# A gated mix of attention and state-space convolution: the written order of all steps replaced by another order

## The chip, the cores and the metric

The kernel runs on one core of a Trainium2 chip. The metric is device time in microseconds (us). The engines are TensorE (PE; its weight loads are shown as PEld), VectorE (DVE), ScalarE (ACT), GpSimd (POOL) and SyncE (SP), whose queue issues all transfers here.

## The reference, cut to what matters

x is 2048 tokens of 512 values. `a` is an attention of 32 heads of 16 dims over four segments of 512 tokens, with a memory carried from segment to segment; `b` is a long convolution of x with a kernel that is computed from state-space parameters; a sigmoid gate for each token mixes them.

```
for s in range(4):                      # segments of 512 tokens
    p = softmax(qs @ ks.T * scale + mask);  a_dot = p @ vs
    a_mem = (phi(qs) @ M) / (phi(qs) @ z + 1e-6)
    o = g * a_mem + (1 - g) * a_dot
    M, z = M + phi(ks).T @ vs, z + sum(phi(ks))
a = concat(o) @ wo
K[d, l] = real(sum_n C[d,n] * exp(dt*A[d,n]*l) * dt*B[d,n])
b = irfft(rfft(x) * rfft(K)) + x * Dskip       # causal, padded to 2L
gate = sigmoid((x * gate_w).sum(-1))
return gate * a + (1 - gate) * b
```

## The kernel before

The kernel first builds a list of 1746 steps (`build_graph`, L525). Each step has a name (its tag), the engine that does it, the tiles that it reads and writes, and a function that emits its instructions. A step is one transfer, one ACT or DVE instruction, or a group of matmuls. Then `replay` (L235) walks through a text, `ORDER` (L368), that was written out beforehand. Each word of it is a step's number; a letter `a` or `v` says that an evacuation, which could be done by ACT or by DVE, is done by ACT or by DVE; the numbers after slashes are the slots of the tiles that this step takes first. `emit` (L264) gives each engine its steps in the order of the text and puts semaphore waits where a step needs another engine's result or a slot that another step must leave. Every engine works through its own list strictly in order, SP's queue of transfers too.

The work is in these parts, which the order interleaves:

* Start. Loads (`ld_*`), transposes of x (`xT0`, L709; later segments by a transposing transfer at L712), preparation of the state-space parameters (`ssm_prep`, L733), which begins with the exponential of `log_dt` on ACT (L750), and twenty powers of a complex vector by repeated squaring (`pow*`, `pwc*`, L784; squares on ACT at L794, sums and products on DVE at L795 and L796).
* Attention, for each segment s and each group hg of 8 heads: projections (`pk`, `pq`, L978), values (`tok`, L917), state of the memory (`st`, `sm`, L936), scores in five pieces (`sc`, L1007) whose exponentials run on ACT over four PSUM banks at once (L1068, 128 x 2048), masks on DVE (`mk`, L1080), products with the values (`pv`, 17 columns each, L1018), normalising (`nrm`, L1036), the memory's part (`mem`) and a transposed sum (`oT`, L1101).
* Tables of the convolution's kernel, for each quarter c of the channels (`tables`, L1137). Two tables F and G are built by complex products on DVE (`tab`, L1165, L1168, L1172) after copies of the first entries (`tabc`). Then the lag products (`lag0` to `lag3`, L1206) multiply them: eight steps for each quarter, each of 32 products of 20 columns with 32 weight loads of 32 columns, followed by two evacuations and four transfers into a table KT. F and G have one slot each (L628, L629), so the tables of the next quarter begin when the lag products of the last have read theirs.
* First level of x's transform (`xl1`, L844), evacuated mostly by ACT, and written to a scratch tensor in memory.
* Convolution in 32 units (`conv`, L1220): a load of constants (`CD`, c_DN in the profile, four slots), second level of x (`X`, loaded as `Zx`, with two swapping transfers), the kernel's transform from KT (`K`, five products of 512 columns), their product on DVE (`Y`, L1281), the inverse (`V`) and a transfer into V2.
* Finals, for 16 blocks of tokens (`finals`, L1297): `fin`, `fir`, `fih`, `fis` on PE, spilled parts (`spl`), and the outputs (`out`).

Evacuations are at L226 (ACT), L227 (DVE), L229 and L230 (with a scale). All matmuls but the transposes share line L686, and all transfers but the transposing ones share L222.

The two lines that make a lag step, and the two that give F and G their single slot:

```
FP = mkpool("F", 10240, 1)
GP = mkpool("G", 16384, 1)
...
i = mm(e, ap(P, sl * NF, n=NF, p0=32 * dq, np_=32), ap(G, (1 - cc) * GPL + (dl // 2) * 2 * NG + dl % 2, [[2, NG]]),
       ap(F, cc * FPL + (dl // 2) * 2 * NF + dl % 2, [[2, NF]]), cc == 0, cc == 1, tile_position=(0, 32 * dq))
```

Of the kernel before, what the change touches and what calls it, by code (L numbers as in the profile page):

```python
# [368 lines left out]
9/0 0/0 205/0 10/1 14/2 23/4/0 15/0 29/0 24v 38/0 54/0 39/1 31/2 30/3 21/0 37/4 12/3 13/4 55/0 33/5 34 35 57/5 36 32/6  # L369
44/7 17/0 40/8 41 377/0 42 45/9 20/0 56v/0 58a 43 11/5 48/0 27/1/1 46/10 47 1/0 49/11 53/0 61/1 50/12 200/6/0/0 62v/0  # L370
59/0 60 378/2 16/0 51/13 28v 52 25/7/2 201a 214/3/0/0 73/2 67/3 63 71/1 72 202 189/0 86v/1 83/2 85/4 22/0 18/0 196/0
197/0 26a 84 87 98v/2 203/1/0 97/5 3/0 95/3 250/4/1/1 253/0/1 74a/3 251a 215 204v 96 107/0 75 254a 240/0/0 99 110v/4
173/6 379 65/1 176/2 109/7 108 174/3 255/1/1/1 241 66 242 111 175/0 1247/1 178/0 77/0 121/2 78/4 119/1 7/0 120
293/2/2/2 179/3 76 193/0 995v/0 177 190 5/0 181/0 64 994v 219/0/1 220 191 88 996v 133/1 256 221 208/0 131/1 132 100
997v 1000/0 999 258 257 122a/5 998v/0 228/0/2 209a 229 210/0 79 206/1 1002 381/0 1003/1 143/2 192/0 198/0 1004 230
211a 144/5 216 145 112 1009/1 1008 158v/6 123 207a 159 1001 223/0/3 252 588/0 134a/7 135 1005 89/1 212/3 213v 294a 295
155/2 1011 1010 90/6 156/0 1226/0 224 225 146a/8 1250/0/0 1251a 799/0 199/0 800/1 157 222/2 1237/3/1 226 227 167a/9
1238a 231 2/0 266/0/1 267 268 801 1012/0 147 1013 1006/1 124 217 232/0 168 160 1020 91 1007 136 1015/0 1248/1 1249a
1014 1252 1021/1 337/0/2 338a 233 236/0/3 148 237 238 334/3/0/0 335a 1016 589/1 169 234/0 1234/0/0 590 1017 1022
1232/2 1018/0 235/1 1233a 1023 262/0/2 1235a 263 1236 264 239 243 101/1 244 1239/3 1240a 1229/2/0 1227/0 271/0/3 272  # L380
1024/1 245/1 1230a 1241 1019 273 1228a 1231 1025 1258/3/1 296/2/0 1026 297a 283/0/0 1259a 284 285 1033/0 1244/0/0
1245a 246 1032 1029 4/0 1034 265/2 1030/1 1035 1260/3 269 270 1261a 103/7 1031 380 279/0/2 280 281 1242/0 1243a
218/3/0 259 260/0 298/3/0/0 299 102 113/2 247 307/0/1 115/2 1036/0 1027/1 114 1262 1028 308 1037 278/0 282 286 287
1268/0 300 309 1246 248/1 249a/0 288/2 125/1 320/0/2 321 274 275/3 1038/1/0 1039 1040 126/1 127 322 137/2 1041 289
1043/3 194 290/1 276 1044 180 1045 1042a 1046 1047a 1263/0/1 1264a 1056v/0 1052v/0 1060 80v/0 339/1/1/1 1055v 138/5
340 1054v 301 1061/1 303/0/0 304 305 394/3/1 383/0/1/1 384a 341 1253/1/0 1254a 395a 324/0/3 342 1062 1053v 325 326 139
1058/0 81 1057 1066 336 302/0 343 400/1/0/0 401 1067/1 306/3 310 1059 311 277 1068 391 116a/2 344 1063 1070/0 346/0/0
1255/2 1073/1 1256a 1257 1069 1072 128v/3 347 348 1074 443/0/1 402 1050/0 1265/2 291/1 1266a 312/0/1 1064/1 292a 149/1
117 1071 444v 1079/0 1078 313 314 1267 349/2 386/0/0 1065 1080 1076/1 150/0 92a/4 490/1/2/2 182 315 316/4 93 387a 1049
1082/0 129 350/0/0 351 491a 398/0 352 82 1081 68a/5 1075 317 319/1 323 1083 152v/1 399a 1289/1 104a/6 355/0/1 356 357  # L390
1090 327 353 105 354 328 396/0 363/0/2 318/0 397a 385 140a/7 329/5 1091/0 330 364 365 358 1077 331 392/3 393a 1284/0/0
94 1286/1 1084 1092 1285a 106 1087 1094/1 367/0/0 368 359/0 1287a 369 1093 493/3/2 492 141 130 494a 1276/0/1 1277a
1085/0 405/0/3 1288 406 407 1095 151 440/1/0/0 441a 1088/1 1086 1297/3/0 1298a 362/0 360 1089 409/0/1 164v/9 410 161/3
118 411 448/1/1/1 366 370 371 372/1 195 1101/3/1 1102 449 373 1051 1103 1104 422/0/2 153 142 390/0 423 442 1105a 445/0
69 374/1 70 1295/3 1096/0 451 1097 450 1098 165 154 424 1296a 1099 361 1299 162/3 1274/1 1100a 1275a 403 426/0/0 427
1114v/0 428 166 163 375/2 1279/3/0 376a 1119/0 1280a 6/0 1281/0 1278 1111v/0 1282a 1118 261 408/1 1112v 412 414/0/3
447/1 1120 602/0 415 416 446 382/1 1113v 1271/2/1 1125/1 1110v 1124 404/3/1 609/0 1116/0 388/1 452 1115 1126 413 417
1117 170v/8 1121 1272a 464/0/1 1122/1 1131/0 171 172 1130 1127 1132 465 418/2 610a 421/2 425 429 1123 430 1128/0 1283
466 419 453 1129 1108 420/1 1269/0 1270a 1273 1292/3/0 1293a 1290/1 1291a 459/0/3 1136 460 431/3 541/0/0 461 542a
1137/1 986/0 1294 1134/0 1300/3/1 1301a 432 1307/1/0 1138 455/0/2 456 457 1133 1302/0 433 1303a 472/0/0 1304 473  # L400
1140/1 1139 1135 1141 1143/0 1308a 183/2 474 538/3/1/1 539a 498/0/0/0 1149/1 184/0 1148 1142 458/1 1150 499 500 462
1146/1 463 1144 1305/2 1306a 1145 1152/0 476/0/2 477 467 478 1151 332/3 333a 1147 1153 1309 468/4 607/2 608a 651/0/0/0
652a 520/0/3 345 469 521 522 471/3 1332/0 597/2/1 598a 475 479 480 1310/0 546/0/1/1 524/0/1 525 1048 547 548 470/0 501
1154/2/0 389 1311/1 549 1155 526 1156 1157 1158a 1106 484/0/5/0 507/0/0 508 481/1 1159/2 540 497/1 482 485 1160 483
495/0 496 486 1161 1162 487 509 1163a 1167 1172v/0 1170v/0 1176 1177/1 1165 434/0/0/1 435 1178 1166 436 1168a 1182
503/0/2 504 1171a 488/3 505 437 1312/2/0 1169v 1183/0 1313a 1173 591 1184 545/0 1174/1 1188 489a/0 1164 605/0 1339/1
506/1 606a 1175 1189/0 512/0/2 513 803 1179 1318/2 532/1/2/0 533 514 502/0 550 510 511 1185 1186/1 534 1187 599/1
562/0/0 563 592 1190 515 551 535 519/0 1368/2 523 1195/1 1194 543/0 516/3 564 603/2 604a 1321/3/1 1322a 1196 1191
570/0/2 571 572 517 438/2 1197 527 528 594/3/2/2 595a 1180/0 1198/1 1181 553/0/3 439a 554 555 1199 704/3/2 705a 1192/0
1314/2 1107 529/4 1315a 1316 1207/1 1193 557/0/1 558 559 1319/3 530 596 1109 1320a 531/0 611/2/0/0 1206 612 518 556/0  # L410
574/0/3 575 576 1208 560 1201/0 561 565 569/1 701/3/1/1 1200 566/1 1209 567 1202 616/0/1 573 1354/1 702a 577 578 568/1
1203 1210/1 1204/0 1211 1205 536/3 617 537a 653 1324 814/0/1 815a 620/0/0 816/3 654/0/0 621 655a 613 625/0/2 626
1212/0/0 1213 579/5 580 581 618 1214 1215 1216a 1325/2 1217/2 988/0 817v 1218 622 637/0/3 638 1219 1220 1221v 1326/1/2
1327v 1328/0 619/3 593/0 1329v 454 601/1 1223 659/2/1/1 660 661 627 623 633/0/1 634 818/1 819v 1426/0 752/0/1 753a 624
628 666/0/0 820/2 1447/1 703 629/0 635 630 667 749/1/2/2 750a 632/0 552 631/0 821v 670/0/2 671 544 582/1/2/1 614 639
583 584 585 636 640 641 662 642/4 615/1/0 658/0 731/0/1 656/0 732 657 672 643 668 1331 663 1330 644 1225 1222 1224
1448/2/0 664 1449v 709/3/0/0 687/0/3 695/0/3/0 710 711 1347/2 1433/2 586/2 696 697 1323 669/3 587v 698 688 751 706/0
707 1450/0 1317 1440/3 673 674 813 757/2/1/1 758 760 683/0/0 759 1441/0/1 684 802 1427/1/2 1428a 685 1442v 1451/2/0
1452a 708/0 1496/1 675/0/2 805/1/0/0 676 1434/0/3 1453/0 1435a 600 806a 1429/1 1443/2 1430/2/1 712 713/4 761 1454/0
1431a 1444/0/2 1445a 689 677 682/1 1350/5/1 1351a 1432 733 678 804/1 1348/2 1349a 686 1361/2 762 763 764/0/2 1446 690  # L420
1436/3 691 679/1 680 692/5 681/1 693 694 1353 1497/0/0 765 645/1/0/1 646 1498a 647 648 768/0/0 769 1335/1/0 1336v
808/0/0 809v 1437/2/3 1362/3/0 1438a 1333/1 1334a 1352 773/0/3 766 774 1363v 1461/3 1355/0/1 1356v 1475/2 649/2 650v/0
1455/1/2 987/1 767/3 1340/0 1456a 770 775 1337 1357/0 1338 1369/1 714/0/2 1358v 1499/0 715 1476/2/1 1477a 1457/1
1364/1 1365a 771 716 699/0 700a 1478/2 772 1390/2 776 1397/0 777/2 778 735/0/0 779/0 1439 1500/2/0 1501v 736 1462/1/3
1463v 1370/0/2 1371a 1479/3/1 1480v 1464/3 780/2 723/0/3 1458/1/2 1459v 1341/0/2 1342v 724 717/3 1343/1 1344a 781/0/2
1482/1 756/1 1483/0/0 725 730/1 734 1359 1468/2 737 738 782 1484v 754/1 1502 1367 1481 739 740/4 741 718/0/1 719 742/1
# [1003 lines left out]
```

## Time and profile before

| what | value |
|---|---|
| median of 3 runs | 317.85 us (317.22 to 318.82) |
| the profiled execution | 314.99 us, of it span 312.8 us |
| granted TensorE clock, mean | 0.947 |
| PE busy | 259.1 us, 4033 matmuls |
| DVE busy | 264.6 us, 641 instructions |
| ACT busy | 262.3 us, 313 instructions |
| matmuls of 20 columns (lag) | 1024, busy 10.2 us together |
| matmuls of 17 columns (pv) | 1280, busy 42.7 us together |
| exponential L1068, 128 x 2048 | 80, mean 1894 ns |

The span runs from the first to the last instruction; the rest of the execution's time lies around it. The page gives busy times of each engine, forty slices with the busy share of each in tenths, and a chain of waits, followed back from the last instruction, in which "issue" is time for which no semaphore accounts. A number in square brackets in the timeline is the idle time of the engine ahead of an instruction, with what ended it.

### The profile page before, as it was taken

The page shows a single profiled execution, that of the slowest core. Times are in us where ns is not written, and L with a number is a line of the kernel's source. Part 1 is how long each engine was busy: PE and PEld are TensorE (multiplying, and loading weights), DVE is VectorE, ACT ScalarE, POOL GpSimd, SP SyncE. Part 2 cuts the span into 40 slices and gives each one's busy share as a digit, 9 for nine tenths or more (in the row PEclk, how much of TensorE's full clock was granted, in tenths as well). Part 3 has the DMA queues.
Part 4 walks back from the last instruction along what each step waited for, and adds up shares of the span by engine and source line. Part 5 has one row for each costly group of instructions (what it writes and reads, how often), then busy time and mean ns, then how long its engine had stood idle before and what let it go on. Part 6 is the DMA issues. An engine that isn't in the chain of part 4 may idle for free.

```text
span 312.8 us, 9547 instructions
## 1 busy us (share of the span) xinstructions
PE 259.1 (83%) x4033; PEld 152.0 (49%) x4078; DVE 264.6 (85%) x641; ACT 262.3 (84%) x313; POOL 3.4 (1%) x9
## 2 busy tenths in 40 slices
PE   1595886658887687979796999999999999999993
PEld 0352443545445553556354655455544455546551
DVE  0799999959999899989996998997988898774473
ACT  2799999959999999899987899997899899986121
POOL 2000000000001000000000000000000000000000
PEclk9997899959999987999978899999999999999998
DMA  5956613400512331413030434675666767352133
GB/s 144 233 172 150 116 53 111 137 4 1 160 22 58 96 103 48 139 25 118 16 94 4 137 107 120 206 207 173 181 204 190 208 182 218 101 154 78 39 129 140
DMA packets 45002, 37.37 MB, mean 119 GB/s; under 512 B 21408, under 2 KB 40864, under 8 KB 44960
## 3 DMA queue, kind: packets, MB, share of 16 engines
q1 hardware_dynamic: 44960, 36.77, 40.7%
q8 instruction: 32, 0.52, 0.7%
q14 instruction: 10, 0.08, 0.1%
HBM read 18.54 MB, written 6.29 MB: 79 GB/s over the span
## 4 chain that ended last, share of the span: by engine, by line
PE 42%; ACT 25%; DVE 19%; DMA 6%; issue 5%; SPq 1%; ACTq 0%; DVEq 0%
PE psum L686 42%; ACT sb L1068 14%; ACT sb L226 7%; DVE sb L1165 5%; DVE sb L1168 4%; DVE sb L1172 4%; ACT sb L794 2%; DMA sb<-c_DN 2%; DMA sb<-sb 1%; DMA sb<-in_B_log_dt_dram 1%; DVE sb L227 1%; DMA scr_Z<-sb 1%; SPq L222 1%; ACT sb L802 1%; DVE sb L1043 1%
## 5 line engine op out<-in xcount | busy, mean ns | idle before, releaser
L686 PE MATMUL psum<-sb 128*128 128x17 bf16 (+11 forms) x3945 | 251.6, 230 | 39.9 <-ACT sb L1068 17.9
L686 PEld LDWEIGHTS psum<-sb 128*128 128x128 bf16 (+3 forms) x3990 | 144.8, 97 | 144.8 <-issue 33.5
L1068 ACT ACTIVATE sb<-psum 128x2048 bf16<-128x2048 f32 x80 | 151.5, 1894 | 7.1 <-PE psum L686 6.3
L226 ACT ACTIVATE sb<-psum 128x512 bf16<-128x512 f32 (+2 forms) x149 | 84.4, 613 | 17.1 <-PE psum L686 15.4
L227 DVE CAST sb<-psum 128x512 bf16<-128x512 f32 (+1 forms) x53 | 35.7, 683 | 11.2 <-PE psum L686 9.5
L1165 DVE TENSOR_TENSOR sb<-sb 128x512 bf16<-128x512 bf16 (+3 forms) x52 | 33.8, 660 | 0.0
L1168 DVE TENSOR_TENSOR sb<-sb 128x512 bf16<-128x512 bf16 (+3 forms) x52 | 33.6, 657 | 0.0
L1172 DVE TENSOR_TENSOR sb<-sb 128x512 bf16<-128x512 bf16 (+3 forms) x52 | 33.5, 659 | 0.0
L1080 DVE TENSOR_TENSOR sb<-sb 128x1024 bf16<-128x1024 bf16 (+1 forms) x40 | 22.3, 575 | 2.8 <-ACT sb L1068 2.8
L1281 DVE TENSOR_TENSOR sb<-sb 128x1024 bf16<-128x1024 bf16 x32 | 21.6, 684 | 0.7 <-issue 0.3
L229 ACT ACTIVATE sb<-psum,sb 128x512 f32<-128x512 f32 (+1 forms) x9 | 5.8, 686 | 9.6 <-PE psum L686 9.6
L1043 DVE TENSOR_TENSOR sb<-psum,sb 128x256 bf16<-128x256 f32 x32 | 13.3, 418 | 0.3
L794 ACT ACTIVATE sb<-sb 128x512 f32<-128x512 f32 x18 | 11.5, 647 | 0.0
L1040 DVE RECIPROCAL sb<-psum 128x16 f32<-128x16 f32 x32 | 8.0, 252 | 3.0 <-PE psum L686 2.8
L227 DVE COPY sb<-sb 128x256 bf16<-128x256 bf16 x18 | 4.9, 287 | 5.6 <-PE psum L686 5.6
L948 ACT ACTIVATE sb<-psum 128x512 bf16<-128x512 bf16 x12 | 7.4, 616 | 2.4 <-PE psum L945 2.4
L230 DVE TENSOR_SCALAR sb<-psum,sb 128x512 bf16<-128x512 f32 (+1 forms) x7 | 5.1, 747 | 4.3 <-PE psum L686 4.3
L1122 DVE TENSOR_TENSOR sb<-psum,sb 128x512 bf16<-128x512 f32 x12 | 8.2, 687 | 0.2
L1338 DVE SCALAR_TENSOR_TENSOR sb<-psum,sb 128x512 bf16<-128x512 f32 x8 | 5.7, 748 | 2.6 <-PE psum L686 2.5
L999 ACT ACTIVATE sb<-sb 128x512 bf16<-128x512 bf16 x12 | 7.5, 635 | 0.0
L796 DVE SCALAR_TENSOR_TENSOR sb<-sb 128x256 f32<-128x256 f32 x18 | 7.4, 418 | 0.0
L795 DVE TENSOR_TENSOR sb<-sb 128x256 f32<-128x256 f32 x18 | 7.3, 415 | 0.0
(67 smaller groups left out, 105.3 us busy)
## 6 DMA issues: line engine op xcount, KB each, us to landing
sb<-sb SPq DMA_DIRECT2D x64, 128.0 KB, 3.2
sb<-c_DN SPq DMA_DIRECT2D x32, 224.0 KB, 2.8
scr_Z<-sb SPq DMA_DIRECT2D x16, 256.0 KB, 2.2
sb<-scr_Z SPq DMA_DIRECT2D x16, 256.0 KB, 3.2
sb<-in_A_x_dram SPq DMA_DIRECT2D x5, 512.0 KB, 5.4
out_dram<-sb SPq DMA_DIRECT2D x8, 256.0 KB, 2.0
sb<-sb SPq DMA_DIRECT2D x20, 64.0 KB, 2.0
sb<-c_M SPq DMA_DIRECT2D x4, 256.0 KB, 4.2
```

What stands on the lines that cost most here:

```text
L226: fa = lambda e: e.activation(dst(), src(), ACT.Copy)
L227: fd = lambda e: e.tensor_copy(dst(), src())
L686: mm = lambda e, o_, l, r_, st, sp, **kw: e.matmul(o_, lhsT=l, rhs=r_, start=st, stop=sp, skip_group_check=True, **kw)
L794: op("ACT", ("As", 512), lambda e, sq=sq, Z=Z: e.activation(ap(sq, n=512), ap(Z, n=512), ACT.Square), r=[Z], w=[sq], key=PW[h] + PWS * k)
L1043: op("DVE", ("V1", 256), lambda e: e.tensor_tensor(ap(o1, gi * 16, [[128, 4], [32, 4], [1, 16]]), ap(T, dims=[[68, 4], [17, 4], [1, 16]]), ...
L1068: o = op("ACT", ("Ax", 2048), lambda e, P=P, pT=pT: e.activation(ap(pT, n=2048), ap(P, n=2048), ACT.Exp, scale=0.25), r=[P], w=[pT])
L1080: op("DVE", ("V2", 128 * nb), lambda e, pT=pT, dims=dims: e.tensor_tensor(ap(pT, dims=dims + [[1, 128]]), ap(pT, dims=dims + [[1, 128]]), ...
L1122: op("DVE", ("V1", 512), lambda e: e.tensor_tensor(ap(o2, 0, [[128, 4], [16, 8], [1, 16]]), ap(P2, 0, [[256, 4], [17, 8], [1, 16]]), ap(R2 ...
L1165: op("DVE", ("V2", 256 * n), lambda e: e.tensor_tensor(run(tile, ne, dst, 1), run(tile, ne, src, sstep), ap(pw, cl * 512, [[2, 128], [0, n ...
L1168: op("DVE", ("V2", 256 * n), lambda e: e.tensor_tensor(run(t2, n, 0, 1), run(tile, ne, src, sstep), ap(pw, cl * 512 + 256, [[2, 128], [0, ...
L1172: op("DVE", ("V2", 256 * n), lambda e: e.tensor_tensor(D_(), D_(), ap(t2, n * 128, [[-n * 128, 2], [2 * n, 64], [1, 2 * n]]), ALU.add), r= ...
L1281: op("DVE", ("V2", 1024), lambda e, Y=Y, XAB=XAB, K3=K3, xo=xo: e.tensor_tensor(ap(Y, dims=[[512, 2], [1, 512]]), ap(XAB, xo, [[512, 2], [ ...
```

## The change

The text `ORDER` is replaced by another one. All 1746 steps, their instructions, memory and transfers stay. What differs is the place of nearly every step in the text, and so the order in which each engine does its own steps; which of ACT and DVE does an evacuation, for 66 of them; and the slots that tiles take. The whole text is 93 lines of numbers; shown are the beginning and the lines around the lag products (steps 1038 to 1046 are lag0's, 1096 to 1104 lag1's, 1154 to 1162 lag2's, 1212 to 1220 lag3's; in each, the fifth is an evacuation), and the end.

```
 ORDER = """
-9/0 0/0 205/0 10/1 14/2 23/4/0 15/0 29/0 24v 38/0 54/0 39/1 31/2 30/3 21/0 37/4 12/3 13/4 55/0 33/5 34 35 57/5 36 32/6
+0/0 10/0 9/1 23/0/0 24v 15/0 29/0 31/0 38/1 32/2 30/3 33/4 13/2 14/3 27/4/1 39/5 37/6 34 35 40/7 54/0 57/1 6/0 36
...
-1268/0 300 309 1246 248/1 249a/0 288/2 125/1 320/0/2 321 274 275/3 1038/1/0 1039 1040 126/1 127 322 137/2 1041 289
-1043/3 194 290/1 276 1044 180 1045 1042a 1046 1047a 1263/0/1 1264a 1056v/0 1052v/0 1060 80v/0 339/1/1/1 1055v 138/5
+298/1/0/0 299 276 248/2 1037 249a/0 114 125/2 320/0/3 321 322 1028 1038/2/0 300 301 289 127/3 290/1 180 1039 1040 336
+1246 126 1041 1042v 139/7 339/1/1/1 340 341 1263/3/0 194 1264a 303/0/2 304 1043/2 1044 277 137/0 1253/3/1 1265/1 138
+342 1045 1046 305 151/4 291/0 1254a 1052v/0 1055v 324/0/0 68v/0 325 1056v/0 1053v 302/3 1054v 1060 343 1061/0 292a
...
-1743/0 1735/3 1736 1737 1738 1744a 1739v 1745
+1675 1742 1743/2 1735/1 1736 1737 1738 1739v 1744a 1745
```

In places of the text: lag0's eight products stand at 337 to 354 before and 337 to 369 after; lag1's at 544 to 572 and 540 to 570; lag2's at 747 to 772 and 739 to 783; lag3's at 935 to 953 and 942 to 979. On SP's queue the load of `log_dt` goes from the fifth place to the fourth, and the first transposing transfer (`xTl1`) from the 11th to the 23rd.

More of the change, by code (lines that the diff above doesn't have):

```diff
@@ L454 @@
[L454 removed]
+0/0 10/0 9/1 23/0/0 24v 15/0 29/0 31/0 38/1 32/2 30/3 33/4 13/2 14/3 27/4/1 39/5 37/6 34 35 40/7 54/0 57/1 6/0 36
+193/0 4/0 41 42 43 44/8 48/0 45/9 46/10 12/4 47 49/11 53/0 50/12 17/0 61/1 59/0 62v/0 51/13 58a/0 60 71/1 52 65/2 11/5
+55/2 56v 73/2 7/0 74v/1 25/3/2 26a 200/5/0/0 201a 250/0/1/1 72 83/3 1247/1 1250/6/0 214/1/0/0 28v 215 75 86v/2 205/0
+85/3 173/4 3/0 21/0 66/5 16/0 253/2/0 84 95/0 178/6 20/0 18/0 97/7 98a/3 1226/0 176/1 1/0 251a 96 107/2 63 181/3
@@ new lines @@
+1248/7 254a 109/0 1249a 22/0 99 110v/4 202 67 189/0 108 377/0 208/3 190 177/0 252 203/0/1 204a 174/0 196/2 255/0/1/1
+191 1251a 119/2 240/0/0 87 79/1 241 120/2 111 209a 122v/5 100 121 123 394/3/1 179/1 256 175 257 133/3 182 88 242
+996v/0 395a 131/2 124 132 219/0/1 220 221 146a/6 77/0 998v/0 134v/7 192/0 1003/0 135 143/3 206/3 76 995v 212/0 1002
+228/0/2 217 64 994v 1004 145/7 997v 213a 112 1008 1009/1 144 216 1252 229 230 78 1010 210/0 211a 1000/0 223/0/3 224
+197/0 198/0 1015/1 147 158v/8 1014 999 136 1016 157/4 207a 235/1 1229/2/1 159 89/2 1001 1012/1 225 222/0 1017 155/3
@@ new lines @@
+1255/3 106 1068 1266a 1267 1063 81 310 311 348 1073/0 400/0/0/0 1069 401 116v/4 1072 443/1/0 1071 1256a 1257 444a
+312/0/1 1074 313 314 386/3/1 402 1078 490/1/2/2 491a 92a/5 349/0 387a 1079/1 1076/0 350/0/2 351 352 1080 1075 1082/1
+1081 385 398/1 399a 149/3 1077 319/3 315 381/0 1083 323 327 328 329/4 355/0/1 356 357 1090 1091/0 396/1 1085/1 397a
+330 316/5 363/0/3 364 152a/8 353 354 365 358 392/1 393a 331/0 359/0 317 1286/3/0 1287a 1084 93 318 1092 1086 5/0
+367/0/0 368 1289/1 150 380 1284/1 369 1064/0 1285a 1288 94 1093 362/3 1094/1 493/2/2 494a 405/0/2 406 407 117 1297/1/1
@@ new lines @@
+1132 414/0/2 415 1129 416 1281/0/0 1273 1133 375/1 1279/2 464/0/1 376a 465 1282a 1134/0 421/1 425 1280a 1137/1 1136
+1135 429 466 1290/0/1 1291a 1283 430 431/3 170a/6 171 417 541/2/1 154 459/0/3 1138 418/2 1122/0 1142 419 542a 432 172
+1140/1 1292/0 1293a 420/1 1139 1294 460 461 1123 1141 1143/0 433 1307/2/0 609/0/0 610a 455/0/0 456 1308a 457 607/0
+1148 608a 1109 1149/1 1300/2/1 1301a 1145 1302/3 1144 472/0/2 473 1303a 474 651/0/1/1 652a 498/2/0/0 499 500 1150
+458/1 2/0 462 1050 463 467 1146/0 1151 476/0/0 1152/1 1305/3 1306a 1147 1304 1309 477 478 1153 597/0/0 538/3/0/0 598a
@@ new lines @@
+1566/2 1567/1/0 1568v 1569/3 874/0/3 875 1530 888 1559/0 1586 1577/2/2 1399/3/0 1400a 1560/0/2 1561a 1578a 855/1
+856a/0 1591/4/0 876 1412/2 907/1 1413/3/2 906 943/5/1/1 937/3/0/1 1381 1401/0 1382 1552/3 1592a 1553/2/3 1562/2 938
+939 1414a 940 1402a 948/0 1544 949 944a 1554a 1555/0 1415/1 1563/3/3 1594/1 1416a 881/0 885 889 890 1564a 1406/2/1
+1407v 865/0/2 866 1495 1593 1595/1/1 1596a 891/1 892 893/0 867 1570/3/1 1408/2 1556/0/0 1409a 1571v 908/0/0 909 1557v
+868/1 872 873 1608/0 1403 877 1404 1597/1 990/2 878/2 879 1609/3/0 1610v 1565 991/0 912/0/2 913 1622/2 1623/0/2 992
@@ new lines @@
+1629/3 1417 945 880 1598/2/3 910 1624v 1418 1625/2 898/3 899v 1599a 1579 914 917/0/1 918 1630/1/3 1626/0/2 1627a
+980/1/3/0 1631v 925/0/3 911/1 915 919 916 981 982 983 926 1601/1 1411 1410 1611/3 1615/2 920 921/4 922 923/1 927
+1419/0 1572 1602/0/1 1603a 1604/0 1628 929/0/0 1612/2/1 1613v 1616/3/2 930 931 1643/0 1558 1422/0/0 1423a 1605/1/2
+1606v 968/0/2 924/2 928 1420/0 1632/1 1617a 932 933 934/5 935 1636/1 19/0 969 1644/3/0 1633/1/0 1600 1421a 951/0/1
+1645a 1618/2 1619/0/3 1424 936 941/2 188 952 1637/3/1 1425 1638a 1634a 955/0/3 956 942v 1682/2 1683/0 953 954/3 993
```

135 lines of the change are left out of this document (53 added, 82 removed).

## The prediction

> **What bounds the kernel now.** I read the page first: busy shares, the 40 slices, the DMA queues, the chain.
>
> ```profile
> PE 259.1 (83%) x4033; PEld 152.0 (49%) x4078; DVE 264.6 (85%) x641; ACT 262.3 (84%) x313; POOL 3.4 (1%) x9
> ...
> PE   1595886658887687979796999999999999999993
> ...
> DVE  0799999959999899989996998997988898774473
> ACT  2799999959999999899987899997899899986121
> ...
> q8 instruction: 32, 0.52, 0.7%
> ...
> PE 42%; ACT 25%; DVE 19%; DMA 6%; issue 5%; SPq 1%; ACTq 0%; DVEq 0%
> ```
>
> No engine is full throughout. VectorE and ScalarE stand at 9 from slice 3 to 23, but for a hole in slice 9; TensorE is full from slice 23 on. The busy times by stage say the same:
>
> ```profile
> 14.00:57.00 43.00, 32.58 (x366) 17.46 (x372) 42.42 (x114) 41.45 (x61) 0.00 (x0) 0.92 0.47 119
> 57.00:72.00 15.00, 10.23 (x355) 7.04 (x354) 11.17 (x36) 11.25 (x14) 0.00 (x0) 0.66 0.24 72
> 72.00:175.00 103.00, 83.18 (x1835) 52.46 (x1849) 96.58 (x231) 95.11 (x112) 1.55 (x2) 0.93 0.24 70
> ...
> 185.00:300.00 115.00, 112.10 (x1247) 61.22 (x1266) 93.17 (x211) 96.80 (x110) 0.00 (x0) 1.00 0.53 156
> ```
>
> (Stretch, length, busy PE, weight loads, DVE, ACT, POOL, then granted clock and DMA.) In the first half DVE and ACT set the pace, after 185 us PE does. Whatever makes DVE and ACT wait before 175 us moves all that follows. The chain of waits, drawn for 55 to 75 us, shows the largest such hole:
>
> ```profile
> 61.19 2.44 PE psum L686 x130
> 63.63 0.73 issue
> 64.36 1.24 PE psum L686 x121
> 65.59 2.22 issue
> 67.81 0.26 PE psum L686 x7
> ```
>
> These are the short products of lag0 (L1206: eight steps, each 32 products of 20 columns with 32 weight loads). PE stands still twice, for nothing that a semaphore shows. VectorE's timeline has the consequence, here and at the next three lags:
>
> ```profile
> 68.09 0.43 DVE L227 COPY sb<-sb 128x256 bf16<-128x256 bf16 x2 [3.47 <-PE psum L686]
> ```
>
> ```profile
> 104.84 0.30 DVE L227 COPY sb<-sb 128x256 bf16<-128x256 bf16 x1 [1.40 <-PE psum L686]
> ```
>
> ```profile
> 137.90 0.43 DVE L227 COPY sb<-sb 128x256 bf16<-128x256 bf16 x2 [0.78 <-PE psum L686]
> ```
>
> ```profile
> 170.93 1.21 DVE L227 CAST sb<-psum 128x320 bf16<-128x320 f32 x2 [2.56 <-PE psum L686]
> ```
>
> The first three are the copy that begins the next table G. F and G have one slot each, so it waits for the last product of the lag before. The sum of these waits is 8.2 us; DVE's other gaps between 57 and 175 us are small.
>
> What the gap is: the instruction queue moved 0.52 MB in 32 packets, and PE and its weight loads are 8,111 instructions, so one packet is about 253 of them. From the end of the first gap to the end of the second is 1.24 + 2.22 = 3.46 us, in which 121 products and as many weight loads ran: one packet. Products that use 250 instructions in less than some 3.5 us wait for the next packet. A lag step takes 0.28 us for its 64 instructions, four steps 1.1 us. A step of 16 products of 17 columns takes 0.40 us for 32, so 250 take 3.1 us; nothing else on PE is as dense.
>
> [...]
>
> **The change, part by part.** No instruction is added or removed. Only places, the engines of 66 evacuations, and slots differ.
>
> *Engines.* Of the evacuations that may go to either, 32 go from ACT to DVE and 34 back, by the two texts; with the small copies from SBUF counted at their own rows (0.42 against 0.66 us), ACT gains about 1.0 us in all and DVE loses 1.3. Cumulated along PE's order the two loads stay within 3 us of the old ones at most marks. I cost it at nothing; bounds -1 and +1.
>
> *Lags spread.* I added the rows' durations of what stands between a lag's first and last product. Before, lag0 has nothing else on PE there; after, it has 1.6 us (a state step, two first-level products, a score step). The other PE work goes from 0.9 to 1.5 us in lag1, 1.1 to 2.6 in lag2, 0.3 to 2.6 in lag3. It matters more that DVE gets work to do meanwhile. From the lag's first product to the G copy, DVE has 2.4 us of work before and 7.0 after in lag0; 3.8 and 5.6 in lag1; 3.5 and 7.4 in lag2; over lag3's own length 2.9 and 5.2. The growth (4.6, 1.8, 3.9, 2.3) is above the wait in each but lag3, where 2.3 stands against 2.56. So DVE's waits would nearly go, if the lag itself takes no longer. It still needs its two packets, so lag0 stays near the 5.5 us it takes now (62.47 to 67.94).
>
> What is late next is ACT. Its gaps at the four places are 2.99, 0.31, none and 2.40 us. The issue pieces on the chain there are 2.95 (0.73 + 2.22), 1.30, 0.62 and 1.71 us. At each place I take the least of chain, DVE and ACT: 2.95 + 0.31 + 0 + 1.71 = 5.0 us saved. Bounds: 0 (see the rivals) and the whole chain, 6.6 us.
>
> *The hand-over to the convolution.* The first K product needs lag3's result through an evacuation and four transfers. By PE work, 7.6 us lie between lag3's last product and that K before, 4.9 after. The way takes 0.45 us of evacuation, four issues of some 0.65 us and a landing (2.2 to 3.6 us in this trace): 5.9 us. So PE would wait 1.0 us where it waits none now. Bounds 0 and 1.7.
>
> *The start.* log_dt is issued fourth on SP's queue instead of fifth, half a microsecond sooner (issues stand 0.5 us apart), and ACT's first exponential waits 5.37 us for it. The transpose that holds SP from 6.16 to 10.99 us moves from the 11th place to the 23rd, so the loads behind it leave up to 4.8 us sooner. Against that, the last copies of x's transposes go behind squares and powers: the K projection starts near 16.3 us by adding the rows, instead of 13.93. ACT has two squares and a 1.0 us copy to fill it. I take 0; bounds -0.9 and +2.4.
>
> *The tail.* The last five products are the same steps, and so are DVE's and ACT's last (out14, out15). V30 and V31 have 6.4 us of PE work between product and first use, against 4.4 and 9.5; landing takes some 3. Nothing, bounds -0.5 and +0.5.
>
> **Sum.** -5.0 + 1.0 = -4.0 us. The profiled execution took 314.99 us (span 312.8 and 2.2 around); 311.0 after. The median shown, 317.85, is 1.0091 times the profiled one, so 313.8 us.
>
> **Rivals.**
> 1. *The gain is eaten in the lags.* A score product put between the lag steps needs four PSUM banks that the last exponential frees, 1.89 us each (L1068). There are six such pairs in the four lags, three more than before. PE works in order, so the lag steps behind it wait, then run as densely as now. If all three cost a whole exponential, 5.7 us come back: 311.0 + 5.7 = 316.7, or 319.6 by the median; with two, 317.6, within 0.5%. For it: PE's waits for L1068 are 17.9 us already. Against it: ACT is busy in that time, and DVE has its new work. Chance 0.17, mostly for no change.
> 2. *Slower: loads for the convolution come late.* SP works in order and each c_DN load waits for its slot. The PE work between the product that lets it go and the one that uses it shrinks for six of them, CD18, 19, 20, 25, 27 and 28: 4.3, 4.7, 3.7, 5.0, 3.7, 4.1 us before, 3.5, 3.9, 3.3, 3.9, 3.5, 3.7 after. PE is 97.5% full there, so each late load is paid in full. It decides from a landing of 4.3 us, where six waits make 4.0 us and the gain is gone. At 4.6 us they make 5.8: 316.8, by the median 319.7. For it: the chain has one such wait of 5.46 us at 209.98. Against: the median landing is 2.8 us, and no byte is added. Chance 0.23, with the start's +2.4 as a smaller form of it.
> 3. *The change doesn't do what it says.* The gap goes with the count of packets, not with density: then the 6.6 us stay, and the hand-over's 1.0 is added, 316.0 or 318.9. Against it: dense places alone show such gaps; where products of 512 columns run, after 185 us, PE is 97.5% busy though packets come there too. Chance 0.08.
>
> **Numbers.** The forecast has 0.52: 313.8 us, own range 310 to 316. The 8-in-10 range takes in the whole chain gain with the earlier start (314.99 - 6.6 - 0.9 + 1.0 is 308.5, or 311.3; a little below for the engines' -1) and rival 2 at 4.6 to 4.9 us: 310.0 to 320.5. A measurement here tells about 0.5% from no change. Faster by more 0.55, within 0.17, slower 0.28.
>
> **What would show it.** The G copy's waits of 3.47, 1.40 and 0.78 us should fall below 0.5; the chain's issue pieces at the lags should shrink from 6.6 to under 2; slice 9's hole should fill; K's first product should come some 4 us sooner. A stretch after 185 us with PE below 95% and c_DN or Zx loads ahead of it would make rival 2 right; a start in which ACT idles after 14 us would make the start's price right.

## The result, and the profile after

The changed kernel takes **304.92 us** (median of 4 runs, 303.17 to 305.48), the one before 317.83 (317.22 to 318.82): ratio 0.958, 95% interval 0.954 to 0.963, so 12.9 us less. Measured again later (experiment 4) it was 304.76 against 315.85, ratio 0.964 (0.959 to 0.969). The forecast was 313.8 us, the range began at 310.0. The direction was right; the gain is three times the one forecast, and the time lies 5 us outside the range. Each ratio and interval here leaves out executions in the chip's slower state, which the medians keep, so a ratio need not be the quotient of two medians.

The profiled executions differ by less: 314.99 before, 305.48 after, 9.5 us. The one before was 2.9 us under its median, the one after 0.6 above. Over all measurements the runs of the old kernel go from 311.8 to 320.3 us, and two executions of one and the same text differ by up to 4.6 us at one step (table below). So no part of a few us can be read from one execution alone.

The page after, the lines that answer to those of before:

```profile
PE 263.6 (87%) x4078; PEld 150.3 (50%) x4078; DVE 264.7 (87%) x639; ACT 263.1 (87%) x315; POOL 3.2 (1%) x9
...
PE   2697698799687888788889999999999999999992
...
DVE  2999999999999998999998799999999869957171
ACT  3999999999999899999989998998899999985321
...
q8 instruction: 32, 0.52, 0.7%
...
PE 52%; DVE 22%; ACT 17%; DMA 4%; issue 2%; SPq 1%; ACTq 0%
```

DVE and ACT work as long as before, in a span that is 9.5 us shorter. Their hole in the ninth slice (5 before) is filled, and the first slice, 0 and 2 before, now shows 2 and 3. "issue" falls from 5% of the chain to 2%, though the instruction queue moves the same 32 packets.

By stretch (length, busy PE, weight loads, DVE, ACT, POOL, then clock and DMA):

```profile
14.00:57.00 43.00, 35.61 (x436) 19.16 (x434) 42.53 (x116) 42.22 (x57) 0.00 (x0) 0.95 0.45 110
57.00:72.00 15.00, 13.84 (x383) 8.50 (x382) 14.61 (x48) 14.97 (x20) 0.00 (x0) 0.80 0.31 96
72.00:175.00 103.00, 86.36 (x1870) 52.74 (x1869) 97.87 (x234) 97.13 (x114) 1.31 (x2) 0.93 0.28 79
...
185.00:300.00 115.00, 112.45 (x1237) 59.92 (x1234) 92.27 (x199) 90.55 (x101) 0.00 (x0) 1.00 0.57 166
```

At lag0 (57 to 72 us) DVE and ACT stand at 14.6 and 15.0 of 15 us, where it was 11.2 and 11.3. After 185 us nothing is changed in kind: PE is busy for 112.45 of 115 us.

The chain at lag0, and VectorE's copies that begin the next tables G:

```profile
58.99 1.21 PE psum L686 x115
60.21 0.54 PE psum L945 x4
60.75 3.39 PE psum L686 x125
```

```profile
64.16 0.43 DVE L227 COPY sb<-sb 128x256 bf16<-128x256 bf16 x2 [0.39 <-PE psum L686]
...
97.90 0.71 DVE L227 COPY sb<-sb 128x256 bf16<-128x256 bf16 x4 [0.65 <-PE psum L686]
...
131.62 0.43 DVE L227 COPY sb<-sb 128x256 bf16<-128x256 bf16 x2
```

The pieces of issue of 0.73 and 2.22 us are gone, and the copies' waits go from 3.47, 1.40 and 0.78 us to 0.39, 0.65 and none.

Where the lead comes from can be read from the same step in both traces. This table is worked out from the traces: start on PE (of the first weight load) of five steps in the kernel before, and how much earlier (-) or later it is in others, one profiled execution each; "again" is a second execution of the same text. Such a difference is time won only where about the same PE work stands ahead of the step in both orders. By the rows' durations that holds here within 0.4 us, but for sc0.1.A1, ahead of which texts with the new head have 1.2 us more.

```
step                 sc0.1.A1  pv0.2.A0  pv1.2.C  sc2.1.B0  pv3.1.A1
before, us               54.4      74.5    145.5     178.1     255.6
after                    -2.7      -7.8     -6.9      -8.6      -9.6
after, again             -3.2      -8.4     -7.3      -9.6     -10.6
new head only            -3.0      -2.9     -3.2      -3.4      -3.9
new head only, again     -3.3      -4.5     -5.9      -8.0      -8.4
new head and lag0        -3.3      -7.4     -5.9      -7.2      -7.9
head and lag0, again     -1.9      -7.0     -6.1      -6.4      -7.0
log_dt only              -1.3       1.4     -0.2      -2.3      -2.8
first 60 words only      -1.1       2.7      1.7       0.2      -0.4
```

In the changed kernel about 3 us are there before lag0 begins, which the forecast did not have. About 5 more come at lag0, 1 us is given back by the time lag2 is over, some 2 come from there to the scores behind lag3, and 1 more after that. The new head alone leads by 3 us at lag0 in both executions; one of them then keeps 3.9 us, the other reaches 8.4.

The clock is a rival that the experiments do not separate. Between 57 and 72 us its granted mean rose from 0.66 to 0.80. In the measurement of experiment 4 it was 0.949 over the eleven runs of the old kernel and 0.974 over the six of the new one. Among the old kernel's own runs a clock higher by 0.01 goes with 0.4 to 1.1 us less, depending on the measurement; by that estimate 1 to 3 us of the gain go with the clock. Whether shorter waits raise the clock, or the clock adds to the gain by itself, no run here shows.

### The profile page after: what moved, and what is told of

It reads as the page before. It is cut to its first block, busy times and chain, and to the rows that moved or that the text cites. A ratio compares the mean times of both kernels' runs of the same rounds, so it can differ in the third digit from the quotient of the medians.

```text
span 303.3 us, 9592 instructions
## 1 busy us (share of the span) xinstructions
PE 263.6 (87%) x4078; PEld 150.3 (50%) x4078; DVE 264.7 (87%) x639; ACT 263.1 (87%) x315; POOL 3.2 (1%) x9
## 4 chain that ended last, share of the span: by engine, by line
PE 52%; DVE 22%; ACT 17%; DMA 4%; issue 2%; SPq 1%; ACTq 0%
PE psum L686 51%; ACT sb L1068 9%; DVE sb L1168 5%; DVE sb L1172 5%; ACT sb L226 4%; DVE sb L1165 4%; DMA sb<-in_A_wo_dram 2%; DMA sb<-in_B_log_dt_dram 1%; ACT sb L794 1%; SPq L222 1%; DMA sb<-sb 1%; ACT sb L948 1%; ACT sb L802 1%; DVE sb L227 1%; DVE sb L1122 1%
## 5 line engine op out<-in xcount | busy, mean ns | idle before, releaser
L686 PE MATMUL psum<-sb 128*32 128x20 bf16 (+11 forms) x3990 | 256.4, 232 | 26.0 <-ACT sb L1068 15.0
L226 ACT ACTIVATE sb<-psum 128x512 bf16<-128x512 f32 (+2 forms) x152 | 86.1, 615 | 6.8 <-PE psum L686 6.2
L227 DVE CAST sb<-psum 128x512 bf16<-128x512 f32 (+1 forms) x50 | 32.9, 674 | 6.1 <-PE psum L686 5.6
L229 ACT ACTIVATE sb<-psum,sb 128x512 bf16<-128x512 f32 (+1 forms) x8 | 5.4, 688 | 13.4 <-PE psum L686 13.4
L230 DVE TENSOR_SCALAR sb<-psum,sb 128x512 f32<-128x512 f32 (+1 forms) x8 | 6.0, 748 | 8.4 <-PE psum L686 8.3
L742 PE MATMUL psum<-sb 128*128 128x128 bf16 x24 | 3.1, 309 | 6.8 <-DMA sb<-in_B_A_re_dram 4.1
```

Source lines behind the costliest of these rows:

```text
L226: fa = lambda e: e.activation(dst(), src(), ACT.Copy)
L227: fd = lambda e: e.tensor_copy(dst(), src())
L686: mm = lambda e, o_, l, r_, st, sp, **kw: e.matmul(o_, lhsT=l, rhs=r_, start=st, stop=sp, skip_group_check=True, **kw)
```

## The experiments

Theory: the lags lose time because PE waits there for instructions (six waits that no semaphore explains, 7.3 us together in the old trace), and the new order hides this; the rest comes from the new head. Rival: what counts is the order in which the other engines get work, and these waits have little to do with it. Each ratio is to the old kernel measured beside it, with its 95% interval.

### 1. Parts of the new order

The texts are cut at places where both hold nearly the same steps, and joined.

```
 ORDER = """
-(places 1 to 334 of the old text)
+(places 1 to 334 of the new text)
 (the steps that are left, as in the old text)
```

is the new head (e1); in the same way new only from 334 to 430, around lag0 (e2), new from 725 on (e3), and new up to 430, head and lag0 together (e7).

> The first 334 places of the new text (up to the step before lag0), then the old text for what is left. In the changed kernel's trace, PE reaches the products of segment 0's last scores 2.7 us sooner than in the old one, because log_dt lands at 6.09 instead of 7.38 us and the sine chain follows. Theory (the start is a gain of its own that everything later keeps): about 2.7 us less than before, 315 us by the median, ratio 0.991. Rival (the start is slack: what follows waits for lag0's packets and its DVE work anyway): no change, ratio 1.000.

> Only the stretch around lag0 in the new order: the old text up to place 334, then the new text's places up to 430, then the old text again. Theory (lag0's two packets, and DVE without work meanwhile, made the hole): 4.8 to 5.6 us less than before, which is what the two traces differ by between 59 and 65 us; ratio about 0.983, and no DVE wait above 1 us at the copy of G after lag0. Rival (the gap goes with the number of packets): ratio 0.995 to 1.000 with the gap still there.

> The old text up to place 725, then the new text: lag2, lag3, the convolution and the finals in the new order. Theory (the start and lag0 made nearly all of the gain): 1 to 2.5 us less than before, ratio 0.992 to 0.997. Rival (the later half holds what the profiled pair does not show, since the medians differ by 12.9 us and the profiled executions by 9.5): 4 us or more less, ratio below 0.988.

> The new text up to the end of lag0's stretch (place 430 of 1746), the old text for the rest: new head and new lag0 together. Theory (both are needed together and the rest of the change brings nothing): 305 to 306.5 us, ratio 0.960 to 0.966 against before, the whole gain. Rival (lags 1 to 3, the hand-over and the convolution's order each add a part of it): 309 to 312 us, as with the new head alone and a part of lag0's 6 us.

Measured: the head 311.38 us, 0.981 (0.975 to 0.987); lag0's stretch alone 315.34, 0.996 (0.991 to 1.000); the later half alone 315.92, 1.001 (0.997 to 1.005); head and lag0 306.78, 0.973 (0.967 to 0.978). So the head, which was costed at nothing, is worth some 6 us, twice what the theory had. lag0's stretch alone misses its expectation: of the issue pieces at lag0 one of 0.36 us is left, as the theory has it, but the time does not follow. In their place PE waits 0.94 and 1.28 us for DVE at lag0, and the copy of G still waits 1.14 us. Steps that the new head had done already now fall into the stretch; whether they take the gain was not tried. The later half brings nothing on the old first half, against both expectations. Head and lag0 come to 8.5 us, less than the whole and more than the head with a part of lag0.

What the head alone leaves at lag0 is seen in PE's timeline of that run:

```profile
59.23 2.21 PE L686 MATMUL psum<-sb 128*32 128x20 bf16 x246 [0.45 <-DVE sb L949]
63.78 0.24 PE L686 MATMUL psum<-sb 128*32 128x20 bf16 x10 [2.34 <-issue]
```

One wait instead of two. Such waits begin at edges that lie 256 instructions apart (last section), and lag0 begins close behind such an edge in both orders, 13 instructions before and 19 here. But PE passed that edge 0.3 us before lag0's first product with log_dt ahead (61.04 and 61.32 us), and 2.1 us before it with the new head (56.95 and 59.02 us, second execution). With the new head lag0's first edge shows no wait. The head's lead (3.0 us at 54 us) goes through.

### 2. Parts of the head

The load of log_dt one place earlier, nothing else:

```
-9/0 0/0 205/0 10/1 14/2 23/4/0 15/0 29/0 24v 38/0
+9/0 0/0 205/0 10/1 15/0 23/4/0 14/2 29/0 24v 38/0
```

and the new text's first 60 words, then the old text (e6).

> The old text with two words exchanged: the load of log_dt goes from the fifth to the fourth place on SP's queue, as in the new text, and nothing else moves. Theory (the 6 us that the new head is worth alone begin at the first exponential, which waits for log_dt, and DVE and ACT carry a lead through to 175 us): the exponential 0.55 us sooner, the time down by 0.5 to 0.6 us. Rival (the lead is lost at the next wait, or the head's gain lies later in the head): 0, within 0.3 us.

> The new text's first 60 words (SP's first loads, the two parts of the parameters' preparation interleaved on DVE and ACT, the first squares and powers), then the old text for all other steps. Theory (the head's gain is the earlier chain from log_dt over the sines to the powers; the sine comes 2.6 us sooner): 2.5 to 4 us less than before, the larger part of the 6 us of the whole head. Rival (the gain comes from the order between 14 and 57 us): less than 1 us.

Measured: 315.97 us, 0.997 (0.993 to 1.002), and 314.94 us, 0.998 (0.994 to 1.003). Neither tells from no change. The first can't decide about the 0.5 us that were expected; the second's interval excludes the expected 2.5 to 4 us, so the theory fell: the start alone is not what the head brings. The table above shows what became of it. Both have a lead of 1.1 to 1.3 us at 54 us, and both have lost it, and more, after lag0. PE's timeline with log_dt ahead, then with the 60 words:

```profile
64.96 1.21 PE L686 MATMUL psum<-sb 128*32 128x20 bf16 x128 [2.49 <-issue]
68.69 0.77 PE L686 MATMUL psum<-sb 128*32 128x20 bf16 x8 [2.52 <-issue]
```

```profile
65.89 1.24 PE L686 MATMUL psum<-sb 128*32 128x20 bf16 x128 [1.52 <-issue]
69.34 0.77 PE L686 MATMUL psum<-sb 128*32 128x20 bf16 x7 [2.22 <-issue]
```

The waits for instructions grew to 5.0 and 3.7 us, from 2.95. The products were ready sooner, but the packet on the instruction queue that follows the edge ahead of lag0 starts at 62.27 us with log_dt ahead, and at 62.15 us before. The 60 words alone also lose their start behind it: up to 14 us DVE and ACT do 8.2 and 8.7 us of work (5.5 and 5.7 before), but from 14 to 30 us only 14.3 and 13.5 of 16: ACT waits 1.7 us there for PE's products and DVE 1.1 us. The whole new head has 15.7 and 15.6 there.

### 3. Fewer instructions in lag0

```
-for cc in range(2):
+for cc in range(1 if c == 0 else 2):
...
```

So lag0's sums have one of their two terms, and the first quarter's kernel of the convolution is not the true one.

> The old text; in lag0 alone, half of the products are left out (the four steps' sums take one of their two terms, so that the first quarter's kernel is not the true one): 128 products with 128 weight loads in place of 256 and 256. Theory (PE stands still there because instructions come no faster than some 250 in 3.46 us): lag0 gets through with about one packet, both pieces of issue (0.73 and 2.22 us) go or nearly, and 3 to 4.5 us are saved. Rival (the products themselves and the order are what cost; code supply costs nothing): half of lag0's own PE time, 1.2 us or less.

Measured: 312.65 us, 0.989 (0.985 to 0.993), 2.6 us by the medians and 3.4 by the ratio. One wait is left at lag0:

```profile
65.42 0.78 PE L686 MATMUL psum<-sb 128*32 128x20 bf16 x8 [1.80 <-issue]
```

The rival's 1.2 us lie outside the interval (1.1% of 316 us is 3.4, the interval 2.1 to 4.7). Half of the instructions in the same order give most of what the theory said, at the low end of its 3 to 4.5 us.

### 4. The parts once more, on one chip

The changed kernel, head and lag0, and the head, unchanged from above.

> The changed kernel itself, on the same chip as the three that follow, so that the parts can be set against it. 305 us; ratio to before 0.958 within its interval. If the gain is smaller here (0.965 or more), a part of the first result came from the chip or the clock.

> The new text up to place 430, the old one for the rest, again, now beside the changed kernel. Theory (head and lag0 together bring two thirds or more, lags 1 to 3 the rest): 1.5 to 4 us above the changed kernel. Rival (the rest of the text brings nothing, as the new later half alone on the old first half brought nothing): within 1 us of it.

> The new text up to place 334, the old one for the rest, again, beside the two. Theory (the new head is worth 3 to 4 us in the trace at 54 us, and what the first call showed beyond that was the chip's spread; lag0's spacing brings 4 to 5 more): 2.5 to 4 us less than before, 4 to 5.5 us more than the text that has lag0 too. Rival (the head is worth the 6 us that were measured at first): 6 us less than before, 2 to 3 more than the text with lag0.

Measured, before being 315.85: the changed kernel 304.76 us, 0.964; head and lag0 307.56, 0.974 (0.969 to 0.979); the head 310.76, 0.975 (0.966 to 0.984), its runs from 305.8 to 314.7. The changed kernel's ratio lies just under the 0.965 from which on a part of the first gain would have come from the chip or the clock; that stays open. By the medians the head is worth 5.1 us, lag0's new stretch 3.2 on top of it, all the rest 2.8. So the head lies between its theory and its rival, and the run with lag0 meets its theory. The head's wide spread (its ratio gives 7.8 us) leaves the split between it and lag0 loose by some 3 us; that the rest brings 2 to 4 us, where the later half alone brought nothing, holds in both measurements of head and lag0.

### 5. Lags bunched again in the new order

lag0's eight products side by side (e4), words of the new text around them:

```
-1028 1038/2/0 300 301 289 127/3 290/1 180 1039 1040 336 1246 126 1041 1042v
+1028 1038/2/0 1039 1040 1041 1043/4 1044 1045 1046 300 301 289 127/3 290/1 180 336 1246 126 1042v
```

and the same with lag1, lag2 and lag3, lag0 left spread (e12).

> The new text with one thing undone: lag0's eight products stand one behind the other on PE, as in the old text, while ACT and DVE keep the new text's order as nearly as the tiles allow. Theory (density on PE makes the gap): the gap of some 2 to 3 us comes back on PE, but DVE keeps its work for that time (7.0 us of it), so 1 to 3 us more than the changed kernel, ratio to before 0.962 to 0.968. Rival (the spacing on PE is all of it): 5 us more than the changed kernel, ratio 0.975. Rival (spacing is nothing, DVE's work all): no more than the changed kernel, ratio 0.958.

> The changed kernel, but in lag1, lag2 and lag3 the eight steps stand next to each other on PE, at the place of the first; lag0 stays spread. Theory (instructions come in blocks of 256, the next one 3.2 to 3.9 us after the last; a bunched lag uses one in 1.2 us, so each bunched lag waits once or twice): gaps at blocks' edges of 0.5 to 2.2 us in each lag, 1.5 to 4 us above the changed kernel. Rival (behind lag0 other engines or waits set the pace and hide it): within 0.8 us of the changed kernel, with the same gaps on PE.

Measured: 311.26 us, 0.980 (0.976 to 0.985), 6.3 above the changed kernel; and 326.35 us, 1.036 (1.030 to 1.041), 21.6 above it. Both theories were far too low; the first run is nearer to the rival that puts all of it, 5 us, on the spacing. The gaps are there as the theory says. PE at lag2 in the second run, then ScalarE and VectorE there:

```profile
129.36 1.21 PE L686 MATMUL psum<-sb 128*32 128x20 bf16 x128 [1.07 <-issue]
133.91 2.32 PE L686 MATMUL psum<-sb 128*32 128x20 bf16 x47 [3.34 <-issue]
```

```profile
135.42 0.63 ACT L999 ACTIVATE sb<-sb 128x512 bf16<-128x512 bf16 x1 [5.00 <-PE psum L686]
```

```profile
135.42 0.30 DVE L1001 TENSOR_SCALAR sb<-sb 128x512 bf16<-128x512 bf16 x1 [4.46 <-PE psum L686]
```

But they come to 8.5 us in the three lags (1.93, 1.07, 3.34 and 2.11), of which the changed kernel has 1.6 too, not to 21. Bunching also moved other products behind the run (score and memory products in the second text), and what that cost is told apart in the next experiment.

### 6. The same orders without the lags' instructions

Each lag step issues 4 products of 80 columns in place of 32 of 20. One of the two terms is left out, and F is read at other places, so the kernel of the convolution is not the true one:

```
-for sl in range(sl0, sl0 + 4):
-    for cc in range(2):
-        for dq in range(4):
-            dl = 32 * dq + 16 * hf + sl
...
+for dq in range(4):
+    dl = 24 * dq
+    i = mm(e, ap(P, sl0 * NF, n=4 * NF, ...), ap(G, GPL + ...), ap(F, ..., [[2, 4 * NF]]), True, True, ...)
```

> The old text; each lag step issues 4 products of 80 columns with 4 weight loads in place of 32 of 20 columns with 32 (only one of the two terms, and wrong places of F: the kernel of the convolution is not the true one). So a lag is 64 instructions in place of 512, and no lag fills a block of 256; the order, all waits and all other work stay. Theory (code supply at the lags is what the old order loses there): the six pieces of issue, 7.3 us, go, with a part of the lag's own PE time: 305.5 to 309 us. Rival (what counts is the order in which the other engines get work; blocks hide it or not): 312 to 315 us.

> The new text with the same 4 wide products in each lag step (the same work left out). Theory: the two gaps left, 1.6 to 2.0 us in all, go: 301 to 303.5 us, and the difference between the old and the new text falls from 11.5 to between 4 and 6 us, the new head's 3 and little else. Rival (order): the difference stays at 9 to 12 us.

> New text to place 334, old text behind, with the wide products in each lag (the same work left out). Theory: with the blocks' gaps gone the head's 3.3 us are all that the new text has: 302 to 305 us, within 1.5 us of the whole new text with wide products. Rival (order): 306 to 310 us.

> New text to place 430, old text behind, with the wide products in each lag (the same work left out). Theory: lag0's new order brings nothing more once its products come in one piece: within 1 us of the run with the head alone. Rival (the order around lag0 is worth its 3 to 6 us without any wait for instructions): 3 us or more below it.

> The text in which lag0's eight steps stand next to each other within the new order, now with the 4 wide products in each lag step (the same work left out as in the other wide runs). Bunching alone had cost 6.3 us. Theory (it cost that because PE waited for instructions there, and others waited for PE): the cost falls below 1.5 us, 303.5 to 305.5 us. Rival (the steps that were moved with it, two state and score products behind the run, cost it): 308 us or more.

> The text in which the steps of lag1, lag2 and lag3 are bunched, now with the wide products in each lag (the same work left out). Bunching had cost 21 us, of which the gaps on PE showed some 7. Theory (code supply and what waits behind it): 305 to 310 us. Rival (the score and memory products that had to change places with it lose most of it): 314 us or more.

```
order                     as it is    with 4 wide products   ratio, wide, to before
old                       317.88      309.85                 0.975 (0.967 to 0.983)
new head, old rest        310.76      305.07                 0.962 (0.955 to 0.969)
new head and lag0         307.56      305.16                 0.964 (0.958 to 0.970)
new                       304.76      304.11                 0.960 (0.955 to 0.966)
new, lag0 bunched         311.26      307.34                 0.971 (0.967 to 0.975)
new, lags 1 to 3 bunched  326.35      318.49                 1.004 (1.000 to 1.008)
```

(Medians in us; those of the first column come from several measurements, with the old kernel's median beside them between 315.23 and 317.88.)

This answers the question in the main. The old order, with every step where it was, gains 8.0 us when most of the lags' instructions go. The new one gains 0.7 by these medians, which come from two measurements; by its two ratios it is between 0.7 us slower and 1.2 faster. PE time is spared too: a lag's eight steps take some 2.2 us without waits and 0.7 with wide products (61.63 to 62.29 us at lag0). At lag0 that time is free in the old order, since with wide products ScalarE works without a gap until the evacuations that begin at 63.83 us, when eight steps of 0.28 us would have ended as well. At the other lags it is argued only, from the new order, which is spared the same PE time and gains next to nothing. So most of the 8 us is the supply; the six waits for instructions on PE in the old trace come to 7.3 us, which agrees. The difference between old and new falls from 11 to 13 us to 5.7, and that is the head: with wide products the head alone, head and lag0, and the whole new text lie within 1.1 us of each other, as the theory had it. The old and the new order themselves lie 0.9 and 0.6 us above the theory's ranges. PE's timeline of the old order with wide products, at lag0:

```profile
60.35 2.01 PE L686 MATMUL psum<-sb 32*128 32x512 bf16 x48 [0.96 <-ACT sb L1068]
64.32 0.61 PE L945 MATMUL psum<-sb 128*128 128x128 bf16 x4 [1.96 <-ACT sb L226]
```

At lag0 no wait is put down to issue any more; PE waits 1.96 us for ScalarE behind it, where it waited 2.95 for instructions. The instruction queue moves 25 packets instead of 32.

The bunched orders answer as well. With wide products they get 3.9 and 7.9 us back (by the ratios 2.8 and 9.8), so of the 6.3 and 21.6 us that bunching cost 3 to 4 and 8 to 10 are supply (with the lags' own PE time in it; the gaps were 8.5), and the rest the steps that were moved with it. The first lies between its theory and its rival. In the second they lose 14 us without any wait of over 0.3 us for instructions: this rival was right on the greater part of that run's loss.

## Why the prediction was wrong in size

*The start: the step that failed.* The forecast put the start at 0, with bounds of -0.9 and +2.4. Measured is a gain of 4.8 to 5.8 us by the medians for the new head (with and without the lags' instructions; by the ratios 4 to 8). The traces show 3.0 to 3.3 us of it at 54 us; where the rest comes from is open. Two things were missed. The first is the row that the forecast itself named, ScalarE's wait for log_dt. Before, on ACT and on DVE:

```profile
7.38 0.63 ACT L750 ACTIVATE sb<-sb 128x512 bf16<-128x512 bf16 x1 [5.37 <-DMA sb<-in_B_log_dt_dram]
...
10.95 1.28 ACT L771 ACT_TABLE_LOAD   x1 [1.62 <-DVE sb L766]
```

```profile
8.12 0.76 DVE L761 TENSOR_TENSOR sb<-sb 128x256 f32<-128x256 bf16 x2 [2.22 <-ACT sb L750]
...
14.21 0.43 DVE L776 TENSOR_TENSOR sb<-sb 128x256 f32<-128x256 f32 x1 [1.09 <-ACT sb L774]
```

After, on ACT and on DVE:

```profile
6.09 0.63 ACT L750 ACTIVATE sb<-sb 128x512 bf16<-128x512 bf16 x1 [4.08 <-DMA sb<-in_B_log_dt_dram]
...
8.04 1.28 ACT L771 ACT_TABLE_LOAD   x1
9.61 0.42 ACT L771 ACTIVATE sb<-sb 128x256 f32<-128x256 f32 x1 [0.28 <-DVE sb L766]
```

```profile
6.75 0.76 DVE L761 TENSOR_TENSOR sb<-sb 128x256 f32<-128x256 bf16 x2 [0.88 <-ACT sb L750]
```

The exponential comes 1.3 us sooner, the table for the sine 2.9. The second thing is that the text also interleaves the two halves of the parameters' preparation on DVE and ACT, so that from there to 14 us ACT waits 0.28 us for DVE and DVE not at all: up to 57 us DVE does 50.3 us of work and ACT 50.5, where it was 47.9 and 47.2. The forecast went through the loads and through PE's start; it weighed PE's first projection, which it put at 16.3 us (13.57 in the trace after). But DVE and ACT set the pace there, by its own first part, and their gaps up to 14 us (the brackets above) were the rows to sum. With the whole new head this lead is kept (-2.9 us or more at every later step of the table); with the old order behind the first 60 words (experiment 2), it is lost. Which steps between word 60 and lag0 make the difference was not tried.

*The lags: the mechanism right, the size somewhat low.* The term was -5.0 us, the least of three engines' gaps at each place. What the supply of instructions cost the old order and not the new is 8.0 less 0.7, or 7.3 us by the wide runs' medians; by the difference that goes when it is taken away (11.1 to 12.9 less 5.7) it is 5.4 to 7.2. The whole chain, 6.6, was the better measure. Taking the least of the three assumed that ScalarE's and VectorE's gaps stay where they were, and that only the smallest is got back; but they are gaps of one cause. In the same-step table lag0 gives about 5 us against 2.95, and behind lag2, with lag3, some 2 against 1.71. Between lag0 and the end of lag2, where 0.31 were to be saved, 1 us goes again. What takes it is not settled: two gaps for instructions are left there (1.07 and 0.54 us), PE's waits for the exponentials are less than before (15.0 against 17.9 us). That the sum of 5.0 us comes as near as it does is in part luck: the places do not agree one by one.

*What was said to show it.* The G copies' waits are 0.39 and 0.65 us and none, where "below 0.5" was said, so one of them misses. The pieces of issue on PE are 1.6 us, for "under 2". The hole in slice 9 is filled. K's first product comes 8.6 us sooner (172.61 against 181.19), for "some 4". lag0 takes 5.1 us from its first product at 58.99 to its last, which ends at 64.06, for "near 5.5".

*Engines of evacuations.* This was costed at 0. ACT's busy time rises by 0.8 us, DVE's by 0.1. Nothing shows a cost.

*The hand-over.* This was costed at +1.0 us. PE's wait for the transfers into KT is 0.4 us. On the chain the last of the four transfers lands in 3.01 us, ahead of the first K:

```profile
169.54 3.01 DMA sb<-sb
...
172.64 1.65 PE psum L686 x21
```

*The tail.* This was costed at 0. From 175 to 300 us PE's listed waits fall from 2.1 us to one of 0.5, for `wo`, and in the table the lead grows by 1.0 us from sc2.1.B0 to pv3.1.A1. So 1 to 1.5 us come from this stretch, which begins long before the tail; they are a part of the 2.8 that the order behind 430 brings.

*Rival 1* (gain eaten in the lags): the score products did not bring the gaps back. *Rival 2* (c_DN late): no wait for c_DN is left on PE, and from 185 to 300 us PE is busy for 112.45 of 115 us. Its price was also too high: at a landing of 4.3 us the old distances of 3.7, 3.7 and 4.1 us would have made 1.4 us of waits too, and only the growth counts. *Rival 3* (packets go with the count): the packets did, the gaps did not; 32 packets cost the old order some 8 us and the new one about 1 at most.

*The median.* The factor 1.0091 was right in kind: the old kernel's profiled execution was low. It left out that the new one's could lie on the other side, 0.6 above; 9.5 between the profiles, 2.8 and 0.6 make the 12.9 between the medians. Where a profiled execution falls within its kernel's spread is luck.

## What to carry to other kernels

Before an order is weighed, sum the gaps of the engines that set the pace, from the first microsecond on, and ask of each whether the new order still has it; a start that "only" moves loads can be one of the large terms. Where one cause makes gaps on several engines at once, its price was here nearer to that of the chain than to the least of them. And the start on PE of one step in two orders can be compared only where the same work stands ahead of it. Breaking up a dense run of short instructions paid here (bunching lag0 again cost 6.3 us, 3 to 4 of them supply), and which steps are moved for it counts as well: of the 21.6 us that bunching lags 1 to 3 cost, 8 to 10 were supply and the rest the steps that were moved with them.

## What the runs showed of the hardware

Instructions of PE are counted here with its products, weight loads and semaphore waits, in the nine profiled executions with products of 20 columns in which every product is recorded. 41 waits of over 0.3 us that no semaphore explains are in them, and all begin at places that leave the same remainder, 194, when divided by 256 (2498 and 3522 in the changed kernel's trace). From one such edge to the next, where PE waited, 2.57 to 4.55 us pass, in the median 3.45; the next packet on the instruction queue starts 1.0 to 1.7 us after such a wait has ended (39 of the 41, the other two 2.1 us). The run with log_dt ahead:

```
instruction   PE passes it at   since the last   of it waiting   packet starts
        962          61.04 us                                         62.27 us
       1218          64.96          3.92 us         2.49 us           66.07
       1474          68.69          3.73            2.52              69.79
```

Why it starts then, no run shows. Where 128 lag products with their loads, which take PE 1.2 us, filled the way from one edge to the next, a wait of 2.2 to 3.3 us followed in these four runs (2.22 before and with the 60 words, 2.52 with log_dt ahead, 3.34 at lag2 with lags 1 to 3 bunched). No stretch from edge to edge that lasted 4.6 us or more ended in such a wait. lag0's first product came 0.3 us after PE had passed the last edge with log_dt ahead, and lag0 waited at both edges that it met; with the new head it came 2.1 us after, and lag0 waited at the second alone.

After 185 us 256 instructions last 8.7 to 14.9 us in the changed kernel's trace, and no such wait follows. At the lags the old order lost some 5 to 8 us by these waits, as far as experiment 6 tells.
